# Softmax sums of two heads on four column quarters of PE, the halves of each sum added by DVE

## The chip, the cores and the metric

The kernel runs on one core of a Trainium2 chip. Five engines work side by side, each through its own instructions in order: PE (matrix multiply; weight loads stand apart in the profile as PEld), DVE (vector), ACT (activation functions and scaled copies), POOL (a second, slower vector engine) and SP, which here only issues DMAs. They wait for each other by semaphores. The metric is the device time of one execution in microseconds (us).

## The reference

Attention over 4 batches of 8 heads (576 tokens, head size 64, with rotary position), and after it a mixture of 8 experts whose gate is normalised by 8 rounds over rows and columns. The change is in the attention:

```python
scores = scale * np.matmul(q_rot, k_rot.transpose(0, 1, 3, 2))
scores = scores - np.max(scores, axis=-1, keepdims=True)
attn = np.exp(scores)
attn = attn / (np.sum(attn, axis=-1, keepdims=True) + 1e-09)
return np.matmul(attn, v).astype(np.float32)
...
logits = x @ w_gate
...
for e in range(E):
    h = np.maximum(x @ w1[e], 0.0)
    ye = h @ w2[e]
    out += P[:, e:e + 1] * ye
```

## The kernel before

Every fp32 operand of a matmul is split into a 16-bit high part and a 16-bit low part, and a product is the sum of three matmuls: high by high, high by low, low by high.

Attention goes over 16 pairs of heads. A pair's two heads lie on the two halves of the partitions (`HEADS`). For each pair PE computes the scores twice: `s_mm` (tile `s`) with queries on the partitions, from which DVE takes the maxima (`mraw`), and `t_mm` (tile `t`) with keys on the partitions, with the maxima subtracted by a further matmul. ACT makes the exponentials of `t` (tile `e`, fp32) and their high half (`eb`); POOL or DVE makes the low half.

`av_mm` is the step that this study is about. A pair has ten: two halves of the queries (288 columns each) by five blocks of keys, 160 in all. The product with V goes to the tile `av` (`po` in the code), the sum of the exponentials over the keys to the tile `as` (`pz`), as a product with a matrix of ones (`one16`). Head 0 uses columns 0 to 63 of PE and partitions 0 to 63 of the result, head 1 the other half, and the two matmuls of such a pair are issued one behind the other. A step has three pairs for `av` (V high by e high, V low by e high, V high by e low) and two for `as` (ones by e high, ones by e low), which accumulate into the same place. In the last block of keys, 64 long, the operands take 64 rows instead of 128.

`av_out` then has ACT copy `as` to `ss` (scaled by 2^12, with a small constant added) and `av` to `x`. 288 sums lie along one partition, and a reciprocal would be long there, so `sums_turn` turns them by way of DRAM, 32 times in all: rows of `ss` to `sd` (step 0), `sd` to the tile `s` with 64 partitions of 9 (step 1), then `av_recip` on DVE, back to `si` (step 2), and from there spread over the partitions as `rs` (step 3). `av_norm` multiplies `x` by `rs`; `x_half` splits the result into `xx`, the input of the experts.

The order of the whole part up to the first expert is made by a planner (`Plan`): each piece of work has an engine, an assumed time (table `US`: `av` for a step of `av_mm`, `r` for `av_recip`), a due time and the pieces it depends on, and the planner lays them out by simulated time. Every engine then runs its list in that order. Expert 0's first two blocks (lines 625 and 646, tile `g`) have late due times, and so fill PE where no attention step is ready. After attention come the gate and the rest of expert 0, up to about 600 us; the other seven experts run from there to the end.

Of the kernel before, what the change touches and what calls it, by code (L numbers as in the profile page):

```python
# [9 lines left out]
F32 = mybir.dt.float32  # L10
F16 = mybir.dt.float16
BF16 = mybir.dt.bfloat16
I32 = mybir.dt.int32
AF = mybir.ActivationFunctionType
ALU = mybir.AluOpType
# [4 lines left out]
P = 128  # L20
# [6 lines left out]
HS = S // 2  # L27
# [17 lines left out]
E_TOP = 10  # L45
# [9 lines left out]
AV_AT = ((3, 0, 0), (3, 0, 1), (4, 0, 2), (5, 0, 3), (6, 0, 4), (7, 1, 4), (8, 1, 0), (9, 1, 1), (10, 1, 2), (11, 1, 3))  # L55

US = dict(
    s=0.48, mx9=0.77, t=0.62, ex=0.84, eh=0.68, av=0.72, mx=1.36, gm=0.4, tt=1.05, ptt=1.4, sc=0.9, hi=0.78, lo=1.04,
    ad=1.12, pro=1.5, mp=0.7, mt=0.2, mr=0.95, n=0.82, d=2.3, r=0.25, x=0.95, xd=0.6, xh=0.44, xl=0.87, xld=0.6, v=0.85, vp=1.2,
    vh=0.84, vl=1.3, f=0.66, fh=0.62, fl=0.72, fc=0.62, w=1.25, wh=0.75, wl=1.0, lm=0.5, le=0.6, ld=6.5,  # L60
)
LATENCY = dict(pe=0.3, act=0.15, dve=0.15, pool=0.2, sp=0.0, none=0.0)
# [91 lines left out]
def attention_moe(ctx, tc, qk, v, trigs, eye, wg, w1, w2, out):  # L154
# [10 lines left out]
    pe, dve, act, pool, sp = nc.tensor, nc.vector, nc.scalar, nc.gpsimd, nc.sync  # L165
# [3 lines left out]
    def mkpool(name, bufs=1, **kw):  # L169
        return tc.alloc_tile_pool(name=name, bufs=bufs, reuse_waits="tile", **kw)  # L170

    dram = mkpool("dram", space=bass.MemoryType.DRAM)
# [6 lines left out]
    att = mkpool("att")  # L179
# [8 lines left out]
    xh, xl = xx[:, 0], xx[:, 1]  # L188
# [53 lines left out]
    idt = att.tile([P, 2, 192], BF16, name="idt")  # L242
    mask = eyes[:, 384:389]
    neg = att.tile([P, P], BF16, name="neg")
    one16 = att.tile([P, 64], F16, name="one16")
    ebias = att.tile([P, 1], F32, name="ebias")
    mbs = [att.tile([P, P], BF16, name=f"mb{i}") for i in range(2)]
    raw, vraw, Z, E, vhl, sc, vs, vmx, mraw, mps, R, avp, avx, inv9 = ({} for _ in range(14))
# [190 lines left out]
    def av_mm(p, qh, jt):  # L439

        first, last = (0, 4) if qh == 0 else (4, 3)
        if jt == first:
            avp[p, qh] = [ps_a.tile([P, 512], F32, tag=t, name=t)[:, 0:HS] for t in ("av", "as")]
        po, pz = avp[p, qh]
        vh, vl = vhl[p]
        e = E[9 * p + (4 if jt == 4 else 5 * qh + jt)]

        def side(j):
            if jt < 4:
                return vh[:, j, jt, :], vl[:, j, jt, :], one16, e[:, 0, j, :], e[:, 1, j, :]  # L450
            r = HEADS[j]
            return vh[r, j, 4, :], vl[r, j, 4, :], one16[r], e[r, 0, qh, :], e[r, 1, qh, :]

        ab = [side(j) for j in range(2)]
        for o, x, y, n in ((po, 0, 3, 0), (po, 1, 3, 1), (po, 0, 4, 2), (pz, 2, 3, 0), (pz, 2, 4, 2)):
            for j, r in enumerate(HEADS):
                pe.matmul(o[r], ab[j][x], ab[j][y], start=jt == first and n == 0, stop=jt == last and n == 2)  # L457

    def av_out(p, qh):
        po, pz = avp.pop((p, qh))  # L460
        x32 = att.tile([P, HS], F32, tag="x32", bufs=4, name="x32")
        s = att.tile([P, HS], F32, tag="ss", bufs=2, name="ss")
        act.activation(s, pz, AF.Copy, bias=1e-9 * 2.0 ** (E_TOP + 12), scale=2.0**12)
        act.copy(x32, po)  # L464
        avx[p, qh] = [x32, s]

    def sums_turn(p, qh, k):

        if k == 0:
            d = dram.tile([2, HS], F32, name=f"sd{p}{qh}")  # L470
            for j in range(2):
                sp.dma_start(out=d[j : j + 1, :], in_=avx[p, qh][1][64 * j : 64 * j + 1, :])
            inv9[p, qh] = d
        elif k == 1:
            t = att.tile([P, 9], F32, tag="s9", bufs=4, name="s9")[0:64]
            sp.dma_start(out=t, in_=inv9[p, qh].rearrange("j (a b) -> (j a) b", b=9))
            inv9[p, qh] = t
        elif k == 2:
            d = dram.tile([64, 9], F32, name=f"si{p}{qh}")
            sp.dma_start(out=d, in_=inv9[p, qh])  # L480
            inv9[p, qh] = d
        else:
            t = att.tile([P, HS], F32, tag="rs", bufs=2, name="rs")
            d = inv9.pop((p, qh)).rearrange("(j a) b -> j (a b)", j=2)
            for j in range(2):
                sp.dma_start(out=t[HEADS[j]], in_=d[j : j + 1, :].to_broadcast([64, HS]))
            avx[p, qh][1] = t

    def av_recip(p, qh):
        t = inv9[p, qh]  # L490
        dve.reciprocal(t, t)

    def av_norm(p, qh, e):
        x32, s = avx[p, qh]
# [184 lines left out]
    def pair_ops(p):  # L679
# [51 lines left out]
        for s, qh, jt in AV_AT:  # L731
            n = 9 * p + (4 if jt == 4 else 5 * qh + jt)
            name, a = f"AV.{p}.{qh}.{jt}", ("AV", (p, qh))
            first = jt == (0, 4)[qh]
            plan.add(
                name, ("pe", US["av"]), 9 * p + s + 0.3, lambda qh=qh, jt=jt: av_mm(p, qh, jt),
                [f"el.{n}", f"vl.{p}"] + ([done] if done else []), allocs=[a] if first else [],
                uses=([] if first else [a]) + [("E", n), ("vhl", p)],
            )
            done = name  # L740
        for j in range(2):
            x = ("xs", (p, j))
            add(f"n{j}", "act", "n", lambda j=j: av_out(p, j), [f"AV.{p}.{j}.{(4, 3)[j]}"], allocs=[x, ("ss", (p, j))], uses=[("AV", (p, j))])
            for k in range(4):
                if k == 2:
                    add(f"r{j}", "dve", "r", lambda j=j: av_recip(p, j), [f"d{j}1"], uses=[("s9", (p, j))])
                plan.add(
                    f"d{j}{k}.{p}", ("sp", US["d"]), at[f"d{j}"], lambda j=j, k=k: sums_turn(p, j, k),
                    [(f"n{j}.{p}", f"d{j}0.{p}", f"r{j}.{p}", f"d{j}2.{p}")[k]],
                    allocs=[[], [("s9", (p, j))], [], [("rs", (p, j))]][k],  # L750
                    uses=[[("ss", (p, j))], [], [("s9", (p, j))], []][k],
                )
            add(f"x{j}", flexible("x", "xd"), 0, lambda e, j=j: av_norm(p, j, e), [f"d{j}3"], uses=[x, ("rs", (p, j))])
            add(f"h{j}", "act", "xh", lambda j=j: x_half(p, j, 0), [f"x{j}"], uses=[x])
            add(f"l{j}", flexible("xl", "xld"), 0, lambda e, j=j: x_half(p, j, 1, e), [f"h{j}"], uses=[x])
# [118 lines left out]
    xd, xt_sb = {}, {}  # L874
# [421 lines left out]
```

## Time and profile before

| | |
|---|---|
| time, median of 3 runs | 1848.56 us (1846.24 to 1852.11) |
| the profiled execution's own time | 1848.74 us |
| its span, first to last instruction | 1846.9 us |
| PE busy in the span | 1750.3 us (95%) |
| DVE busy | 1192.4 us (65%) |
| ACT busy | 666.1 us (36%) |
| POOL busy | 471.5 us (26%) |

Rows that follow below are of five kinds. A table by stretch gives each engine's busy time with the number of instructions. A timeline gives start and length of merged instructions; the length of a matmul is modelled and includes its way through the array, so the distance between starts tells what it holds. A row by line or tile gives a group's count, busy time and mean, or its shortest, middle and longest duration. A wait is total us, times, longest us. A shape such as 128*64 in a matmul row is rows by columns of the array that it uses.

### The profile page before, as it was taken

The numbers are of one execution on the slowest core, as the hardware profiler recorded it, in microseconds if no ns is written. First come the engines' busy times: TensorE is split into PE (matmuls) and PEld (weight loads), VectorE is DVE, ScalarE is ACT, GpSimd is POOL, SyncE is SP. The second block draws the span as 40 slices with busy tenths as digits, with TensorE's granted clock in tenths as the row PEclk, the third lists the DMA queues.
The fourth block names the chain that finished last, engine by engine and source line by source line (L and its number), as shares of the span: only waits on it lengthen the run. The fifth ranks groups of instructions, "written<-read, shape, count | busy, mean of one in ns | idle before, by whom it ended". The sixth has DMA issues, their size and how long they took to land.

```text
span 1846.9 us, 32936 instructions
## 1 busy us (share of the span) xinstructions
PE 1750.3 (95%) x13920; PEld 1108.9 (60%) x13920; DVE 1192.4 (65%) x1909; ACT 666.1 (36%) x1121; POOL 471.5 (26%) x388
## 2 busy tenths in 40 slices
PE   3886899899999899999999999999999999999999
PEld 1544445555445566666666666666666666666665
DVE  8998899874680756564656564746475656656543
ACT  1774767677231422232223231313222222222221
POOL 2865667652221302020201010202021120101000
PEclk9998999999999999999999999999999999999999
DMA  5122212200110322131222222121222222222223
GB/s 195 59 89 87 72 56 66 91 15 15 52 64 17 108 76 93 57 103 60 95 75 75 86 69 82 68 92 67 83 69 81 80 81 69 72 89 72 78 80 92
DMA packets 45460, 140.06 MB, mean 76 GB/s; under 512 B 10304, under 2 KB 14720, under 8 KB 41216
## 3 DMA queue, kind: packets, MB, share of 16 engines
q1 hardware_dynamic: 45312, 137.96, 22.4%
q8 instruction: 109, 1.79, 0.4%
q14 instruction: 39, 0.32, 0.1%
HBM read 128.35 MB, written 9.58 MB: 75 GB/s over the span
## 4 chain that ended last, share of the span: by engine, by line
PE 74%; DVE 14%; DMA 5%; ACT 4%; issue 2%; POOL 1%; SPq 1%; DVEq 0%; POOLq 0%; ACTq 0%
PE m L1071 31%; PE m L1055 27%; PE g L646 4%; PE g L625 4%; PE s L379 2%; DVE mraw L380 2%; PE av L457 2%; DMA rs<-si 2%; PE t L424 1%; DMA wraw<-in_w 1%; DVE w1l L229 1%; DVE h L1096 1%; PE as L457 1%; DVE Z L229 1%; DMA si<-s 1%
## 5 line engine op out<-in xcount | busy, mean ns | idle before, releaser
L1071 PE MATMUL m<-w2h,h 128*128 128x512 f16 x2016 | 640.6, 379 | 0.0
L1071 PEld LDWEIGHTS <-h 128*128 128x128 f16 x3024 | 293.7, 98 | 302.4 <-issue 0.3
L1055 PEld LDWEIGHTS <-w1h 128*128 128x128 f16 x3920 | 369.7, 98 | 102.7 <-issue 12.3
L1071 PE MATMUL m<-w2l,h 128*128 128x512 f16 x1008 | 382.1, 379 | 0.0
L1055 PE MATMUL m<-ts,w1h 128*128 128x256 f16 (+1 forms) x2240 | 349.1, 262 | 2.7 <-DVE u L1087 2.7
L1087 POOL TENSOR_TENSOR c<-u,t 128x512 f32<-128x512 f32 (+1 forms) x70 | 82.6, 1180 | 814.6 <-DVE u L1087 722.2
L1055 PE MATMUL m<-ts,w1l 128*128 128x256 f16 (+1 forms) x1120 | 284.6, 262 | 0.0
L1092 ACT ACTIVATE h<-c 128x512 f16<-128x512 f32 (+1 forms) x210 | 117.2, 582 | 460.8 <-DVE c L1087 424.9
L1055 PE MATMUL m<-xx,w1h 128*128 128x256 f16 (+1 forms) x1680 | 263.0, 263 | 8.3 <-ACT m L1084 8.3
L1055 PE MATMUL m<-xx,w1l 128*128 128x256 f16 (+1 forms) x840 | 214.0, 263 | 0.0
L1096 DVE SCALAR_TENSOR_TENSOR h<-c,h 128x512 f16<-128x512 f32 (+1 forms) x210 | 143.1, 704 | 102.0 <-ACT h L1092 101.5
L1055 PEld LDWEIGHTS <-w1l 128*128 128x128 f16 x1960 | 192.0, 98 | 18.0
L435 POOL TENSOR_TENSOR eb<-e,eb 128x576 f16<-128x576 f32 x109 | 153.0, 1405 | 111.9 <-ACT eb L432 55.2
L1079 DVE SCALAR_TENSOR_TENSOR accA<-m,pp,accA 128x512 f32<-128x512 f32 x168 | 125.3, 746 | 74.7 <-PE m L1071 74.4
L428 ACT ACTIVATE e<-t,ebias,pc 128x576 f32<-128x576 f32 x144 | 119.7, 831 | 82.5 <-PE t L424 81.2
L379 PE MATMUL s<-Z 64*128 64x288 f16 (+1 forms) x960 | 92.3, 306 | 48.5 <-DVE mraw L380 42.2
L1079 DVE SCALAR_TENSOR_TENSOR accB<-m,pp,accB 128x512 f32<-128x512 f32 x84 | 63.0, 750 | 111.8 <-PE m L1071 111.8
L380 DVE TENSOR_REDUCE mraw<-s 128x2 f32<-128x576 f32 x144 | 107.3, 745 | 20.4 <-PE s L379 19.7
L1087 DVE TENSOR_TENSOR c<-m,u 128x512 f32<-128x512 f32 (+1 forms) x140 | 88.8, 634 | 38.7 <-PE m L1055 38.7
L1084 ACT COPY t<-m 128x512 f32<-128x512 f32 (+1 forms) x70 | 37.9, 541 | 205.0 <-PE m L1055 205.0
L432 ACT CAST eb<-e 128x576 f16<-128x576 f32 x144 | 96.6, 671 | 3.8
L457 PE MATMUL av<-eb,vh 128*64 128x288 f16 (+1 forms) x640 | 91.0, 301 | 6.9 <-ACT x L464 4.7
(148 smaller groups left out, 2205.4 us busy)
## 6 DMA issues: line engine op xcount, KB each, us to landing
ts<-xd SPq DMA_DIRECT2D x110, 512.0 KB
wraw<-in_w SPq DMA_DIRECT2D x28, 1024.0 KB
raw<-in_qk SPq DMA_DIRECT2D x32, 576.0 KB
ts<-xd SPq DMA_DIRECT2D x28, 256.0 KB
vraw<-in_v SPq DMA_DIRECT2D x4, 1280.0 KB
rs<-si SPq DMA_DIRECT2D x64, 72.0 KB
wraw<-in_w SPq DMA_DIRECT2D x8, 512.0 KB
xd<-ts SPq DMA_DIRECT2D x8, 512.0 KB
```

What stands on the lines that cost most here:

```text
L379: pe.matmul(po[j], zz[r, x, qc], zz[r, y, QH[kh]], start=n_ == 0, stop=n_ == 2)
L380: return lambda: dve.reduce_max(o, ps[:, :, 0:HS], axis=AX.X)
L428: act.activation(e32, ps[:, :, 0:HS], AF.Exp, bias=ebias, scale=sc[p][0])
L432: act.copy(E[g][:, 0], e32)
L435: engine[e].tensor_tensor(E[g][:, 1], e32, E[g][:, 0], op=ALU.subtract)
L457: pe.matmul(o[r], ab[j][x], ab[j][y], start=jt == first and n == 0, stop=jt == last and n == 2)
L1055: pe.matmul(live[bk][:, f * w : (f + 1) * w], x[:, a, i, fs], y[:, i], start=first and f == 0 and n == 0, stop=n == 5, skip_group_check=True,)
L1071: pe.matmul(po, x, y[:, ch], start=n == 0, stop=n == 11)
L1079: dve.scalar_tensor_tensor(o, pt.pop((th, j)), pp[e, hf][:, tt : tt + 1], o, op0=ALU.mult, op1=ALU.add)
L1087: engine[e_].tensor_tensor(temp(n, tag), live[x], live[y], **add)
L1092: act.activation(t[:, 0 : 2 * w], live[src], AF.Relu)
L1096: dve.scalar_tensor_tensor(f(hq[n][:, 1]), live[src], 0.0, f(hq[n][:, 0]), op0=ALU.max, op1=ALU.subtract)
```

## The change

`av_mm` keeps the three pairs for `av`. For `as`, the ones get 32 columns instead of 64, and the four products (high and low half of e, two heads) each get a quarter of the columns of their own: high half of head 0 and 1 on partitions 0 and 32, low half on 64 and 96. They are no longer accumulated into each other, so four rows leave `ss` instead of two, the tile `s` has two halves of 64x9, and `av_recip` adds them with the small constant in one scalar_tensor_tensor before the reciprocal. The factor 2^12 moves, as 2^-12, from the copy of the sums to the copy of `av`. In the planner's table `av` goes from 0.72 to 0.62 and `r` from 0.25 to 0.45.

```diff
-    s=0.48, mx9=0.77, t=0.62, ex=0.84, eh=0.68, av=0.72, mx=1.36, gm=0.4, tt=1.05, ptt=1.4, sc=0.9, hi=0.78, lo=1.04,
-    ad=1.12, pro=1.5, mp=0.7, mt=0.2, mr=0.95, n=0.82, d=2.3, r=0.25, x=0.95, xd=0.6, xh=0.44, xl=0.87, xld=0.6, v=0.85, vp=1.2,
+    s=0.48, mx9=0.77, t=0.62, ex=0.84, eh=0.68, av=0.62, mx=1.36, gm=0.4, tt=1.05, ptt=1.4, sc=0.9, hi=0.78, lo=1.04,
+    ad=1.12, pro=1.5, mp=0.7, mt=0.2, mr=0.95, n=0.82, d=2.3, r=0.45, x=0.95, xd=0.6, xh=0.44, xl=0.87, xld=0.6, v=0.85, vp=1.2,
...
-    one16 = att.tile([P, 64], F16, name="one16")
+    one16 = att.tile([P, 32], F16, name="one16")
...
-        for o, x, y, n in ((po, 0, 3, 0), (po, 1, 3, 1), (po, 0, 4, 2), (pz, 2, 3, 0), (pz, 2, 4, 2)):
+        for x, y, n in ((0, 3, 0), (1, 3, 1), (0, 4, 2)):
             for j, r in enumerate(HEADS):
-                pe.matmul(o[r], ab[j][x], ab[j][y], start=jt == first and n == 0, stop=jt == last and n == 2)
+                pe.matmul(po[r], ab[j][x], ab[j][y], start=jt == first and n == 0, stop=jt == last and n == 2)
+        for t in range(2):
+            for j in range(2):
+                g = slice(64 * t + 32 * j, 64 * t + 32 * j + 32)
+                pe.matmul(pz[g], ab[j][2], ab[j][3 + t], start=jt == first, stop=jt == last)
...
-        act.activation(s, pz, AF.Copy, bias=1e-9 * 2.0 ** (E_TOP + 12), scale=2.0**12)
-        act.copy(x32, po)
+        act.copy(s, pz)
+        act.activation(x32, po, AF.Copy, scale=2.0**-12)
...
-            d = dram.tile([2, HS], F32, name=f"sd{p}{qh}")
-            for j in range(2):
-                sp.dma_start(out=d[j : j + 1, :], in_=avx[p, qh][1][64 * j : 64 * j + 1, :])
+            d = dram.tile([2, 2 * HS], F32, name=f"sd{p}{qh}")
+            for g in range(2 * 2):
+                sp.dma_start(out=d[g // 2 : g // 2 + 1, g % 2 * HS : g % 2 * HS + HS], in_=avx[p, qh][1][32 * g : 32 * g + 1, :])
...
-            t = att.tile([P, 9], F32, tag="s9", bufs=4, name="s9")[0:64]
-            sp.dma_start(out=t, in_=inv9[p, qh].rearrange("j (a b) -> (j a) b", b=9))
+            t = att.tile([P, 2, 9], F32, tag="s9", bufs=4, name="s9")[0:64, 0:2]
+            sp.dma_start(out=t, in_=inv9[p, qh].rearrange("t (x b) -> x t b", b=9))
...
-        dve.reciprocal(t, t)
+        dve.scalar_tensor_tensor(t[:, 0], t[:, 0], 1e-9 * 2.0**E_TOP, t[:, 1], op0=ALU.add, op1=ALU.add)
+        dve.reciprocal(t[:, 0], t[:, 0])
```

Since the planner's table has changed, all engines get another order. On PE, in the fifth pair of heads, a step ended before (`as` is the tile of the sums, `one_106` the ones, `s` and `Z` the scores of another pair):

```order
L457 LDWEIGHTS one_106
L457 MATMUL as<-eb,one_106 64x288
L379 LDWEIGHTS Z
L379 MATMUL s<-Z 128x288
L379 LDWEIGHTS Z
L379 MATMUL s<-Z 128x288
```

At the same place of PE's list the changed kernel has (`vh` and `vl` are V's halves, `av` the product's tile):

```order
L461 LDWEIGHTS one_106
L461 MATMUL as<-eb,one_106 32x288
L457 LDWEIGHTS vh
L457 MATMUL av<-eb,vh 64x288
L457 LDWEIGHTS vh
L457 MATMUL av<-eb,vh 64x288
```

The sums now fill 32 partitions instead of 64, and the next step of `av_mm` follows directly, where scores stood between the two.

On DVE, in the first turn of sums, the list of before reads (`R` and `g` belong to the maxima, `wmx` to expert 0's weights):

```order
L405 TENSOR_SCALAR R<-g,eyes 128x64
L226 TENSOR_REDUCE wmx<-wraw 128x1
L491 RECIPROCAL s_673<-s_673 64x9
L380 TENSOR_REDUCE mraw<-s 128x2
L320 TENSOR_TENSOR raw<-raw 128x576
```

and that of the change, at the same place:

```order
L405 TENSOR_SCALAR R<-g,eyes 128x64
L226 TENSOR_REDUCE wmx<-wraw 128x1
L495 SCALAR_TENSOR_TENSOR s_678<-s_678 64x9
L496 RECIPROCAL s_678<-s_678 64x9
L380 TENSOR_REDUCE mraw<-s 128x2
L320 TENSOR_TENSOR raw<-raw 128x576
```

One instruction has come ahead of the reciprocal, and the maxima stand behind both.

On SP's queue, the second turn of the first pair was issued as

```order
L472 DMA sd_782<-ss 1x288 x2
L476 DMA s_822<-sd_782 64x9
L480 DMA si_875<-s_822 64x9
L486 DMA rs<-si_875 64x288 x2
L253 DMA raw<-in_qk 128x1152 x2
```

and is now issued, with the loads of a later pair's q and k (`raw`) inside it, as

```order
L476 DMA sd_835<-ss 1x288 x4
L480 DMA s_892<-sd_835 64x2x9
L253 DMA raw<-in_qk 128x1152 x2
L484 DMA si_944<-s_892 64x9
L490 DMA rs<-si_944 64x288 x2
```

Four rows go out instead of two, and the write-back of the reciprocals stands behind the loads.

## Rows read from the trace of the kernel before

**Rows 1.** Busy us (and instructions) of each engine by stretch, in us.
```profile
core 0: us, PE busy (x) PEld busy (x) DVE busy (x) ACT busy (x) POOL busy (x), PEclk, DMA share, GB/s
40.00:180.00 140.00, 105.56 (x1282) 67.30 (x1282) 128.19 (x194) 89.93 (x142) 94.73 (x70) 0.94 0.23 77
180.00:300.00 120.00, 110.77 (x1171) 59.48 (x1171) 107.05 (x160) 82.48 (x131) 73.58 (x57) 0.96 0.21 64
300.00:460.00 160.00, 151.71 (x1777) 85.92 (x1773) 118.04 (x193) 116.35 (x184) 86.84 (x67) 1.00 0.13 44
460.00:600.00 140.00, 137.26 (x744) 69.15 (x741) 73.52 (x159) 38.83 (x71) 29.07 (x24) 1.00 0.13 44
```

**Rows 2.** Expert 0's first matmuls, line 625: shortest, middle, longest ns; first, last start.
```profile
L625 PE MATMUL g<-xx,wh x130: 376/379/634, 180.1 to 476.2; 128*128 128x512 f16 x130
```

**Rows 3.** The chain that ended last, by line: 40 to 180, then 300 to 460 us.
```profile
by line: DVE mraw L380 10.9%; DVE Z L229 6.9%; DMA rs<-si 6.4%; issue 5.2%; DMA s<-sd 5.1%; DMA si<-s 5.1%; DVE wmx L226 4.9%; DVE vl L229 4.3%; DVE ctok L289 4.2%; ACT e L428 4.0%; DVE mb L390 3.8%; DVE wl L229 3.8%; PE s L379 3.7%; DVE mb
...
by line: PE av L457 14.6%; PE t L424 10.6%; PE g L625 10.2%; PE s L379 9.6%; PE as L457 7.4%; DMA rs<-si 6.2%; PE t L421 5.6%; PE g L646 4.1%; DMA sd<-ss 4.0%; DMA s<-sd 3.8%; DVE mraw L380 3.1%; DMA si<-s 3.1%; ACT e L428 2.0%; DVE vl L229
```

**Rows 4.** PE's waits, 40 to 180 us: total us, times, longest.
```profile
PE s L379 <- DVE mraw L380: 16.1, 12, 4.1
```

**Rows 5.** Tile as by stretch: PE busy, ACT busy (instructions), clock, DMA share, GB/s.
```profile
40.00:180.00 140.00, 22.22 (x200) 3.99 (x10) 0.94 0.23 77
180.00:300.00 120.00, 16.72 (x160) 3.22 (x8) 0.96 0.21 64
300.00:460.00 160.00, 28.60 (x280) 5.25 (x13) 1.00 0.13 44
```

**Rows 6.** Timeline of PE, two steps and what follows: start, length in us.
```profile
342.41 0.29 PE L457 MATMUL av<-eb,vh 128*64 128x288 f16 x2
...
343.39 0.41 PE L457 MATMUL as<-eb,one 128*64 128x288 f16 x4
343.73 0.54 PE L379 MATMUL s<-Z 64*128 64x288 f16 x6
```

**Rows 7.** Timeline of PE, from 128 to 64 columns.
```profile
186.86 0.59 PE L625 MATMUL g<-xx,wh 128*128 128x512 f16 x2
187.29 0.38 PE L625 MATMUL g<-xx,wl 128*128 128x512 f16 x1
187.60 0.31 PE L457 MATMUL av<-eb,vh 128*64 128x288 f16 x2
187.75 0.29 PE L457 MATMUL av<-eb,vl 128*64 128x288 f16 x2
```

**Rows 8.** Timeline of PE, from 64 to 128 columns.
```profile
456.20 0.41 PE L457 MATMUL as<-eb,one 128*64 128x288 f16 x4
456.54 0.60 PE L625 MATMUL g<-xx,wh 128*128 128x512 f16 x2
```

**Rows 9.** DVE's small operations: busy us, mean ns; durations of two of them.
```profile
L386 DVE TENSOR_TENSOR mm<-mraw 128x9 f32<-128x9 f32 x16 | 9.4, 589 | 0.6
L390 DVE TENSOR_TENSOR mb<-mm,mb 128x18 bf16<-128x18 f32 x16 | 8.3, 519 | 0.6
...
L390 DVE TENSOR_TENSOR mb<-mm,mb x16: 180/182/1326, 41.8 to 433.3; 128x18 bf16<-128x18 f32 x16
L491 DVE RECIPROCAL s<-s x32: 193/198/207, 66.5 to 465.7; 64x9 f32<-64x9 f32 x32
```

**Rows 10.** The turn of sums: row DMAs on SP (ns); DVE's wait; SP's wait.
```profile
L472 SPq DMA_DIRECT2D sd<-ss x64: 218/245/387, 59.0 to 461.0; - x64
...
DVE s L491 <- DMA s<-sd: 8.6, 3, 3.5
...
SPq L480 <- DVE s L491: 136.6, 32, 8.6
```

**Rows 11.** ACT's two copies of a turn: busy us, mean ns.
```profile
L463 ACT ACTIVATE ss<-as 128x288 f32<-128x288 f32 x32 | 12.9, 402 | 3.4 <-PE as L457 3.4
L464 ACT COPY x<-av 128x288 f32<-128x288 f32 x32 | 12.5, 391 | 0.0
```

More of the change, by code (lines that the diff above doesn't have):

```diff
@@ L479, in sums_turn @@
             d = dram.tile([64, 9], F32, name=f"si{p}{qh}")
-            sp.dma_start(out=d, in_=inv9[p, qh])
+            sp.dma_start(out=d, in_=inv9[p, qh][:, 0])
             inv9[p, qh] = d
```

## The prediction

> **What bounds the kernel now.** The changed lines run only in the attention part, the first 460 us. So I first asked which engine holds the clock there, with a table of busy time by stretch [rows 1]. Before 180 us DVE is busy 128.19 of 140 us and PE 105.56: DVE leads. From 180 to 300 us the two are level (PE 110.77, DVE 107.05 of 120). From 300 to 460 us PE is busy 151.71 of 160 and DVE 118.04, and from 460 to 600 PE is busy 137.26 of 140. The turn comes at 180.1 us, where the first matmul of expert 0 runs [rows 2]: from there PE has work with no deadline to put between attention steps, so what attention saves on PE becomes earlier filler and a shorter end. The chain that ended last says the same [rows 3]: in the first stretch it runs mostly over DVE lines and over the DMAs of the sums (rs, sd, si: 16.6% together), in the later one over PE's av, t, g, s and as. In the first stretch PE's largest wait is for DVE's maxima, 16.1 us [rows 4]. The time therefore has two prices: PE time counts after 180 us, DVE time before it.
>
> How many changed pieces lie in each stretch I read from the matmuls into `as` [rows 5]: 200, 160 and 280, at four a step, are 50, 40 and 70 of the 160 steps; the copies that empty `as`, 10, 8 and 13, are the turns of sums.
>
> **PE: what goes.** A step issues five pairs of matmuls, each pair on two halves of the columns. From 342.41 to 343.39 us two steps without a break start eight pairs in 0.98 us, 0.1225 us a pair [rows 6]. The change puts the two pairs of sums into one group of four. If the four run side by side as the two of a pair do, a step loses one pair: 160 x 0.1225 = 19.6 us in all, 110 x 0.1225 = 13.5 us after 180 us.
>
> **PE: what comes.** The sums now use 32 columns, the products 64, so the shape of the array in use changes inside each step. The trace shows what other changes of shape cost. Two pairs of `as` from 343.39 should end their turn at 343.39 + 0.245 = 343.635; the next shape, 64 rows by 128 columns, starts at 343.73: 0.095 us lost [rows 6]. Where only columns change, the same: two 512-column matmuls take 0.43 us from 186.86 to 187.29, so one more should free PE at 187.505, and the 64-column pair starts at 187.60 (0.095); its successor comes 0.15 later instead of 0.1225, as its weights were not ahead (0.025 more) [rows 7]. The way back, 64 to 128 columns, is 456.20 + 0.245 = 456.445 against 456.54 (0.095) [rows 8]. No row shows 64 to 32, so its bounds are 0 and 0.096 us. I take the upper: rows 7 and 8 change columns alone, and no neighbour of theirs is cheaper.
>
> The Trainium skill says it as a rule ("TensorEngine Tiling (Array Packing)", Tiling Modes, Key Properties): changing the tiling mode, not just the tile, drains the engine. By that rule, too, the upper bound holds; by the same page's speed-up of up to four for at most 32 columns alone, the step would just be a pair shorter. The rows on 64 and 128 columns agree with the first; none shows 32.
>
> Counting changes of shape down the two PE orders to the last step gives 443 before and 638 now: 195 more. One lies inside each of the 160 steps; the rest are mostly the 32 places where a step follows another directly, as in the shown piece, and PE must return from 32 to 64 columns. 195 x 0.096 = 18.7 us, and 32 x 0.025 = 0.8 us for weights: 19.5 us. Against 19.6 us saved, PE's sum is 0, and after 180 us (110 of 160) it is 0 as well.
>
> **DVE: what comes.** Each of 32 turns gets a scalar_tensor_tensor on 64x9 that adds the halves, ahead of the reciprocal. The reciprocal's row is no good price: it reads one tensor and always takes 193 to 207 ns. The nearest rows with two tensors in SBUF are 128x9 and 128x18: means 589 and 519 ns, and for the latter a median of 182 with a maximum of 1326 [rows 9]. The size of the data is nothing; something is sometimes waited for inside the instruction. Bounds: 0.18 and 1.33 us; I take 0.52, the mean of the row on the smallest operation that resembles it.
>
> The Trainium skill ("VectorE: DVE Perf Modes", Two Vector instructions with no wait between them) has an instruction with two SBUF tensors read the second through an interface shared with GpSimd; rows 9 agree, and POOL is busy 94.73 of 140 us in the first stretch. Priced by the reciprocal the edit would be 0.2 us a turn, by this row 0.52.
>
> Ten turns before 180 us are 5.2 us of DVE. DVE idles 8% there, partly in waits that the order can fill, so I count 3. Eight more up to 300 us are 4.2 us beside a PE as loaded; I count 1. The remaining 14 are hidden by PE (95% busy, DVE 74%). With the bounds: 10 x 0.18 = 1.8 us, nearly all hidden, up to 10 x 1.33 + 8 x 1.33 / 4 = 16 us.
>
> **The turn of sums.** Four row DMAs leave SP instead of two, 0.245 us each, so s lands 0.5 us later [rows 10]; the fetch of 64x2x9 has twice the pieces. DVE comes later than the data in 29 of 32 turns: it waited for them 3 times, 8.6 us. And SP waits for the reciprocal 136.6 us over 32 turns, 4.3 each, longer than a landing. So the half microsecond shows only where DVE stands waiting: 0.5 us in all, 1.5 if twice as many turns are late. Behind the waiting instruction stand DVE's maxima, and behind these PE's scores. In SP's new order two loads of q and k stand between the fetch and the write-back of the second turn, and wait there for a free buffer; the planner does this in few places, and four x buffers cover it.
>
> **ACT.** Scale and bias move from one copy to the other; with them it takes 402 ns, without 391 [rows 11]: nothing, as the two swap.
>
> **Sum.** 1848.74 us (the profiled execution, span 1846.9, 0.2 above the median of 1848.56) + 0 (PE) + 4 (DVE) + 0.5 (turn) = 1853.2: **1853 us**, +0.2%. A measurement of this kernel tells about 0.3%, 5.5 us, from no change.
>
> **Rivals.** (1) *Faster: 64 to 32 columns costs nothing.* If the 32-column groups count as parts of the 64-column halves, 13.5 us of the 19.6 arrive (the first 50 steps run where PE has slack): 1853 - 13.5 = 1839.5. For it: no row shows this pair of shapes. Against it: rows 6 to 8, one price for every pair. It decides where a change costs under 0.02 us: (0.096 - 0.02) x 134 changes after 180 us are the 10 us that part 1853 from 1843. Chance 0.20. (2) *The four don't run side by side*, but as two pairs, and the change doesn't do what it says: the saving is gone and the changes of shape stay: 1853 + 13.5 = 1866. Against it: two side by side are plain in rows 6. Chance 0.08. (3) *The two-tensor add meets POOL nearly each time* and costs 1.2 to 1.3 us: +14 us instead of 4, 1863. POOL is busy 68% of the first stretch, so it may. Chance 0.12. (4) *The new order*: the planner prices a step at 0.62 and puts 318 matmuls of expert 0 before the last step, not 270. PE stands idle 9 + 8 us from 180 to 460; if half of that is filled, 1853 - 8 = 1845. Chance 0.10. My own case has 0.50, alone 1847 to 1860.
>
> **Chances.** Faster by over 0.3% (below 1843): 0.16 of rival 1, 0.05 of my case, 0.04 of rival 4: 0.25. Slower (above 1854): 0.08 of rival 2, 0.11 of 3, 0.17 of my case: 0.36. Within: 0.39. The range 1839 to 1866 cuts about half of rivals 1 and 2 and the tail of 3, some 0.17.
>
> **What would show it.** In the new PE timeline the group of four should start 0.22 us after the last pair of products (0.12 would be rival 1), and what follows it 0.22 later (0.34 would be rival 2). PE's busy time to 460 us hardly shows it, since starts count. The row of the new add should have a mean near 0.52 with a median near 0.19. The first matmul of expert 0 should come 3 to 4 us later than 180.1. If that start comes no later, my DVE term is wrong; if the stretch from there to 600 us changes by over 5 us, my PE term is.

## The result and the profile after

The changed kernel takes 1865.67 us (median of 5 runs, 1863.75 to 1867.95), the kernel before 1849.23 (5 runs): a ratio of 1.0083, 95% interval 1.0060 to 1.0106. On 1849 us that is 15.3 us slower; the forecast was 4.5 slower, in a range that ended at 1866, 0.3 us above the measured time. The profiled execution took 1867.95 us, its span is 1866.1.

The table by stretch answers to [rows 1].

```profile
40.00:180.00 140.00, 106.58 (x1256) 61.39 (x1256) 124.48 (x185) 90.50 (x140) 97.27 (x72) 0.89 0.23 77
180.00:300.00 120.00, 108.16 (x1070) 51.40 (x1066) 105.94 (x167) 75.54 (x121) 65.40 (x52) 0.96 0.20 62
300.00:460.00 160.00, 146.08 (x1638) 72.23 (x1638) 126.68 (x200) 103.71 (x163) 79.79 (x65) 0.96 0.15 43
460.00:600.00 140.00, 137.94 (x907) 68.57 (x906) 91.91 (x184) 55.91 (x99) 32.41 (x25) 1.00 0.14 48
```

Up to 300 us no engine is much busier, and from 300 to 460 us only DVE is (126.68 us for 118.04). Yet in each of the first three stretches PE gets through fewer matmuls (1256 for 1282, 1070 for 1171, 1638 for 1777), and 907 instead of 744 are left for the fourth: attention advances more slowly. The granted clock is lower in the first stretch (0.89 for 0.94) and the third (0.96 for 1.00): PE was at 1.2 GHz for more of the time.

The group of four in PE's timeline, between the last pairs of products and what follows it:

```profile
274.22 0.29 PE L457 MATMUL av<-eb,vl 128*64 128x288 f16 x2
274.34 0.29 PE L457 MATMUL av<-eb,vh 128*64 128x288 f16 x2
274.56 0.31 PE L461 MATMUL as<-eb,one 128*32 128x288 f16 x4
274.80 0.39 PE L651 MATMUL g<-wh,hh 128*128 128x512 f16 x1
```

The pairs of products are 0.12 us apart, and the four start together 0.22 after the last: 0.0975 us beyond a pair's 0.1225. The change from 64 to 32 columns costs what the others cost. What follows starts 0.24 later, not 0.34 or more: the four do run side by side, and the way out costs 0.1175 us, 0.02 more than in [rows 8].

The new add and the reciprocal (shortest, middle, longest ns), expert 0's first matmuls, and the rows that leave `ss`, which answer to [rows 9], [rows 2] and [rows 10]:

```profile
L495 DVE SCALAR_TENSOR_TENSOR s<-s x32: 150/156/1360, 66.8 to 500.0; 64x9 f32<-64x9 f32 x32
L496 DVE RECIPROCAL s<-s x32: 206/207/208, 67.9 to 500.2; 64x9 f32<-64x9 f32 x32
...
L630 PE MATMUL g<-xx,wh x320: 272/379/634, 185.3 to 591.1; 128*128 128x512 f16 x128, 128*128 128x256 f16 x32
...
L476 SPq DMA_DIRECT2D sd<-ss x128: 212/249/439, 60.1 to 494.9; - x128
```

The add's usual length is 0.156 us and its longest 1.36; its mean, in the view by line, is 0.466 us:

```profile
L495 DVE SCALAR_TENSOR_TENSOR s<-s 64x9 f32<-64x9 f32 x32 | 14.9, 466 | 4.9 <-DMA s<-sd 4.9
```

Expert 0 starts 5.2 us later than in [rows 2], where 3 to 4 were forecast. The last sums of attention reach `ss` and leave it at 494.9 us, where [rows 10] has 461.0; 48 more matmuls of expert 0 come ahead of them in the new order, 48 x 0.215 = 10 us of the 34. The other 24 us were not taken apart.

### The profile page after: what moved, and what is told of

Same layout as the page of the kernel before. It is cut to its first block, busy times and chain, and to the rows that moved or that the text cites. A ratio compares the mean times of both kernels' runs of the same rounds, so it can differ in the third digit from the quotient of the medians.

```text
span 1866.1 us, 33078 instructions
## 1 busy us (share of the span) xinstructions
PE 1763.8 (95%) x13920; PEld 1090.6 (58%) x13920; DVE 1215.3 (65%) x1944; ACT 666.9 (36%) x1121; POOL 463.1 (25%) x385
## 4 chain that ended last, share of the span: by engine, by line
PE 60%; DVE 3%; ACT 1%; issue 1%; DMA 1%; POOL 0%
PE m L1076 32%; PE m L1060 28%; DVE w1l L229 1%; DVE h L1101 1%; DMA wraw<-in_w 1%; DVE accA L1084 0%; ACT h L1097 0%; DVE wmx L226 0%; DVE c L1092 0%; ACT w2h L233 0%; ACT accA L876 0%; POOL c L1092 0%; DVE u L1092 0%; ACT w1h L233 0%; ACT m L1089 0%
## 5 line engine op out<-in xcount | busy, mean ns | idle before, releaser
L1092 POOL TENSOR_TENSOR c<-u,t 128x512 f32<-128x512 f32 (+1 forms) x70 | 81.9, 1171 | 815.2 <-DVE u L1092 721.8
L435 POOL TENSOR_TENSOR eb<-e,eb 128x576 f16<-128x576 f32 x102 | 143.0, 1404 | 102.5 <-ACT eb L432 74.7
L457 PE MATMUL av<-eb,vh 128*64 128x288 f16 (+1 forms) x640 | 95.2, 312 | 6.6 <-POOL eb L435 3.6
```

The lines of the kernel that those rows point to most:

```text
L435: engine[e].tensor_tensor(E[g][:, 1], e32, E[g][:, 0], op=ALU.subtract)
L457: pe.matmul(po[r], ab[j][x], ab[j][y], start=jt == first and n == 0, stop=jt == last and n == 2)
L1092: engine[e_].tensor_tensor(temp(n, tag), live[x], live[y], **add)
```

## The experiments

Theories: A, the changes of shape on PE (with the add and the turn) cost what the result shows in any order; B, the planner's new order does; C, PE's time is covered and the longer turn of sums costs it; D and E, two readings of why an add of 9 numbers a partition costs so much. Ratios are to runs of the kernel before on the same chip, with the 95% interval; us are that ratio on 1849. The ratio is not that of the two medians, so the two can differ by a microsecond or two.

**The old order.** The changed kernel with the planner's old table.

```diff
-    s=0.48, mx9=0.77, t=0.62, ex=0.84, eh=0.68, av=0.62, mx=1.36, gm=0.4, tt=1.05, ptt=1.4, sc=0.9, hi=0.78, lo=1.04,
+    s=0.48, mx9=0.77, t=0.62, ex=0.84, eh=0.68, av=0.72, mx=1.36, gm=0.4, tt=1.05, ptt=1.4, sc=0.9, hi=0.78, lo=1.04,
```

(and `r` from 0.45 back to 0.25). Expected: 

> The changed kernel with the planner's old table (av 0.72, r 0.25), so that every engine runs the order of before, with the new group of four and the new add in their places. Theory A (the changes of shape, the add and the turn cost what the result shows, whatever the order): 1860 to 1868 us. Theory B (the planner's new order, made with a step priced too low, costs most of it): 1849 to 1854 us. Changes of shape counted down PE's order to the last step: 626, against 443 before.

Measured: 1861.88 us, 1.0068 (1.0055 to 1.0080), +12.6 us. The order is not the main cause.

**The new order alone.** The kernel before with the new table (`av` 0.62, `r` 0.45). Expected: 

> The kernel before with the new table alone (av 0.62, r 0.45): old matmuls, old turn, the order of the changed kernel. Theory A: 1849 us, within 4. Theory B: 1860 to 1868 us.

Measured: 1851.95 us, 1.0014 (1.0005 to 1.0024), +2.6 us. Theory B holds for a sixth of the loss.

**A pair less, nothing else.**

```diff
-        for o, x, y, n in ((po, 0, 3, 0), (po, 1, 3, 1), (po, 0, 4, 2), (pz, 2, 3, 0), (pz, 2, 4, 2)):
+        for o, x, y, n in ((po, 0, 3, 0), (po, 1, 3, 1), (po, 0, 4, 2), (pz, 2, 3, 3)):
...
-                pe.matmul(o[r], ab[j][x], ab[j][y], start=jt == first and n == 0, stop=jt == last and n == 2)
+                pe.matmul(o[r], ab[j][x], ab[j][y], start=jt == first and n in (0, 3), stop=jt == last and n in (2, 3))
```

Expected: 

> The kernel before without the pair that sums the low halves of the exponentials (it leaves the low half out of the softmax sums): a step of four pairs, no change of shape inside, old turn, old table. This is what the change would give if a change of shape cost nothing. If PE's time counts after 180 us as predicted: 110 x 0.1225 = 13.5 us less, 1832 to 1839 us. If PE's time is hidden in attention: 1846 to 1850 us.

Measured: 1845.69 us against 1848.56 before, 0.9993 (0.9980 to 1.0007): -1.3 us, not to be told from nothing. This fell out against the prediction: 19.6 us less of PE's work, of which 13.5 after 180 us, bring at most 4.

**All in quarters.** No change of shape inside a step: V's products too go out in groups of four.

```diff
-            for j, r in enumerate(HEADS):
-                pe.matmul(po[r], ab[j][x], ab[j][y], start=jt == first and n == 0, stop=jt == last and n == 2)
+            for j in range(2):
+                for h in range(2):
+                    g = slice(64 * j + 32 * h, 64 * j + 32 * h + 32)
+                    pe.matmul(
+                        po[g], ab[j][x][:, 32 * h : 32 * h + 32], ab[j][y], start=jt == first and n == 0,
+                        stop=jt == last and n == 2,
+                    )
```

Expected: 

> The changed kernel with the old table, and the products with V as well in quarters of the columns: each pair of 64 columns becomes four matmuls of 32 columns, so a step is four groups of four and the shape doesn't change inside it. Theory A (the change inside the step is what eats the saved pair): the pair saved after 180 us is 13.5 us, the turn and the add still cost some 5: 1836 to 1846 us. If groups of four don't run side by side, or sixteen issues hold PE up: over 1866 us. If the loss sits in the turn and the add instead: 1855 us and more.

Measured: 1861.95 us, 1.0078 (1.0065 to 1.0092), +14.4 us. Taking the changes of shape out of the steps brought nothing, where theory A allowed 1846 at most; theory A falls, and the loss is to be looked for in the turn.

**Changes of shape alone.** The sums accumulate as before, by two groups of four in place of two pairs.

```diff
-                pe.matmul(o[r], ab[j][x], ab[j][y], start=jt == first and n == 0, stop=jt == last and n == 2)
+                for g in [r] if x < 2 else [slice(64 * j + 32 * h, 64 * j + 32 * h + 32) for h in range(2)]:
+                    pe.matmul(o[g], ab[j][x], ab[j][y], start=jt == first and n == 0, stop=jt == last and n == 2)
```

Expected: 

> The kernel before with the two pairs for the sums issued as two groups of four matmuls of 32 columns that accumulate as before: five turns of PE a step as before, plus a change of shape inside each step; old turn, old table. PE's own bill is 183 changes of 0.096 us in and some 0.02 more on the way out: 20 us. Theory A (changes of shape carry the loss): 1860 to 1868 us. Theory C (PE's time is covered in attention, as the run without a pair showed, and the longer turn of sums with its add on DVE carries the loss): 1848 to 1854 us.

Measured: 1859.51 us, 1.0052 (1.0040 to 1.0064), +9.6 us. The time lies just below theory A's range and well above theory C's. More work on PE does cost, where less brought nothing: about half of the 20 us added arrives.

**The turn alone.** Matmuls as before, four rows, the larger fetch, the add (a scalar_tensor_tensor, which here reads two tensors).

```diff
-            d = dram.tile([2, HS], F32, name=f"sd{p}{qh}")
-            for j in range(2):
-                sp.dma_start(out=d[j : j + 1, :], in_=avx[p, qh][1][64 * j : 64 * j + 1, :])
+            d = dram.tile([2, 2 * HS], F32, name=f"sd{p}{qh}")
+            for g in range(2 * 2):
+                sp.dma_start(out=d[g % 2 : g % 2 + 1, g // 2 * HS : g // 2 * HS + HS], in_=avx[p, qh][1][32 * g : 32 * g + 1, :])
...
-        dve.reciprocal(t, t)
+        dve.scalar_tensor_tensor(t[:, 0], t[:, 0], 1e-9 * 2.0 ** (E_TOP + 12), t[:, 1], op0=ALU.add, op1=ALU.add)
+        dve.reciprocal(t[:, 0], t[:, 0])
```

Expected: 

> The kernel before with the new turn alone: matmuls as before, four rows out of ss, the fetch of 64x2x9, and the add on DVE (the two halves are here two copies of the whole sum, the scale is half). Old table. Theory C: 1858 to 1864 us. Theory A: 1849 to 1853 us.

Measured: 1859.40 us, 1.0060 (1.0048 to 1.0072), +11.1 us: theory C.

**The rows alone.** The same without the scalar_tensor_tensor. Expected: 

> As the run with the new turn alone, without the add on DVE: four row DMAs and the larger fetch, the reciprocal of one half. If the DMAs carry theory C's loss: 1855 to 1862 us. If DVE's add carries it: 1848 to 1851 us.

Measured: 1850.15 us, 1.0010 (1.0001 to 1.0019), +1.8 us.

**The add alone.** The old turn, with a scalar_tensor_tensor that adds a tile of zeros.

```diff
-        dve.reciprocal(t, t)
+        dve.scalar_tensor_tensor(t, t, 0.0, zero9[0:64], op0=ALU.add, op1=ALU.add)
+        dve.reciprocal(t, t)
```

Expected: 

> The kernel before with a scalar_tensor_tensor on 64x9 ahead of each reciprocal, which adds a tile of zeros: the turn's DMAs as before. By the rows of the changed kernel it takes 0.47 us on average, 32 times, 15 us of DVE. If DVE's add carries theory C's loss: 1855 to 1862 us. If the DMAs carry it: 1848 to 1852 us.

Measured: 1859.81 us, 1.0052 (1.0039 to 1.0065), +9.6 us. The add carries most of the turn's price: rows and add measured apart make 1.8 + 9.6 = 11.4, against 11.1 measured together, within the intervals.

**The turn with a reduction.** The add as an operation that reads one tensor.

```diff
-        dve.scalar_tensor_tensor(t[:, 0], t[:, 0], 1e-9 * 2.0 ** (E_TOP + 12), t[:, 1], op0=ALU.add, op1=ALU.add)
-        dve.reciprocal(t[:, 0], t[:, 0])
+        u = att.tile([P, 9], F32, tag="u9", bufs=4, name="u9")[0:64]
+        dve.reduce_sum(u, t.rearrange("p t b -> p b t"), axis=AX.X)
+        inv9[p, qh] = u
+        dve.reciprocal(u, u)
```

Expected: 

> The run with the new turn alone, with the add done by a tensor_reduce over the two halves into a tile of its own, which reads one tensor, instead of the scalar_tensor_tensor on two. Theory D (the add's price is DVE's wait for POOL inside an instruction that reads two tensors): the add falls from 0.39 to about 0.17 us, and with it 11 us of loss to some 5: 1852 to 1856 us. Theory E (the price is that of any further instruction between the landing and the reciprocal): 1858 to 1862 us.

Measured: 1855.45 us, 1.0049 (1.0035 to 1.0064), +9.1 us. In its trace, and in that of the add alone:

```profile
L492 DVE TENSOR_REDUCE u<-s x32: 155/158/168, 66.4 to 471.1; 64x9 f32<-64x18 f32 x32
```

```profile
L492 DVE SCALAR_TENSOR_TENSOR s<-s,zero x32: 149/154/1381, 68.7 to 476.3; 64x9 f32<-64x9 f32 x32
```

The two operations have the same usual length; only the one that reads two tensors is ever long, up to 1.38 us. In the run with the add alone each of the ten adds over 0.2 us started while a tensor_tensor of POOL was running and ended 0.02 us after it, as here:

```profile
338.52 1.27 POOL L436 TENSOR_TENSOR eb<-e,eb 128x576 f16<-128x576 f32 x1
```

```profile
338.98 0.83 DVE L492 SCALAR_TENSOR_TENSOR s<-s,zero 64x9 f32<-64x9 f32 x1 [4.61 <-DMA s<-sd]
```

(A bracket holds how long the engine stood idle before, and what ended it.) The other 22 met no instruction of POOL, one that started after them, or the last 0.12 us of one. Eleven of the 32 reductions started in the middle of a tensor_tensor of POOL, and took 0.155 to 0.167 us. That part of theory D is shown. But the time fell by only 2 us of the expected 6 against the run with the new turn, inside what the intervals allow for nothing (1855.45 lies in theory D's range only because this chip's runs of before are faster, 1846.60).

**The whole change with a reduction**, in the old order (the same edit in the changed kernel). Expected: 

> The whole change in the old order (old table), with the add done by a tensor_reduce. The same run with the scalar_tensor_tensor was 12.6 us over before. Theory D: 5 to 7 us less than that, 1854 to 1858 us. Theory E: 1860 to 1863 us.

Measured: 1855.76 us, 1.0044 (1.0031 to 1.0056), +8.1 us, 4.5 less than with the scalar_tensor_tensor. Each of the two differences, 2.0 and 4.5, is uncertain by over 3 us. By their mean the wait for POOL is some third of the add's price, a rough share; the rest stays with an instruction of 0.16 us that waits for nothing inside. Theory D and theory E each hold in part. Whether an instruction elsewhere in DVE's list would cost as much was not run.

**The matmuls of the change alone.** The kernel before with the change's matmuls: old order, old turn, the scale and constant of before. Against the changed kernel, in the turn:

```diff
-            for g in range(2 * 2):
-                sp.dma_start(out=d[g // 2 : g // 2 + 1, g % 2 * HS : g % 2 * HS + HS], in_=avx[p, qh][1][32 * g : 32 * g + 1, :])
+            for j in range(2):
+                sp.dma_start(out=d[j : j + 1, :], in_=avx[p, qh][1][32 * j : 32 * j + 1, :])
...
-        dve.scalar_tensor_tensor(t[:, 0], t[:, 0], 1e-9 * 2.0**E_TOP, t[:, 1], op0=ALU.add, op1=ALU.add)
```

Expected: 

> The matmuls of the change alone, in the old order: three pairs and one group of four, but only the two rows of the high halves leave ss, by the old turn without an add (it leaves the low halves out of the softmax sums). Prediction's PE bill: saved 19.6, changes of shape 17.6, their weights and way out some 4: +2 us of PE work, and so 1848 to 1852 us. If a change of shape costs more than its gap (by other instructions that come late, or by the clock): 1854 to 1860 us.

Measured: 1848.71 us against 1846.60 before, 1.0009 (1.0000 to 1.0019), +1.7 us.

**All in quarters, old turn.** Expected: 

> As the run before in this list, with the products with V in quarters as well, so that no shape changes inside a step: four turns of PE, old turn, low halves left out of the sums. If PE's work is what counts, as in the run without a pair: 1844 to 1848 us. If sixteen matmuls of 32 columns cost something of their own (their issue, or the clock): 1850 us and more.

Measured: 1846.75 us, 0.9996 (0.9984 to 1.0007), -0.7 us. Sixteen matmuls of 32 columns a step cost nothing that the time shows, and bring nothing. In the trace their groups of four start 0.12 us apart (223.35, 223.47, 223.60), as pairs do. With the turn's 11.1 us this makes 10.4, where the run with both had 14.4; that these 4 us are more than chance is not shown, and what they would be stays open.

## Why the prediction was right, and where its sizes were off

The forecast of 1853 was short by 12.5 us, and the prediction's own case, 1847 to 1860, does not hold the time. That the whole range does, by 0.3 us, is luck: its end of 1866 is the time of rival 2, whose mechanism is not there. What failed is the step that hides the add on DVE, above all behind PE from 300 us on: 4 us were let through for it, and it costs 9 to 10.

The bill adds up from parts that were run by themselves: matmuls 1.7, turn 11.1 (of which rows 1.8, so 9.3 for the add), order 2.6: 15.4 us, against 15.3 measured. In the old order the first two make 12.8, against 12.6. Each part is uncertain by some 2 us and the whole by 4, so that they agree to a tenth is chance.

**PE's sum: right within 3 us of PE's work.** It was forecast at 0. Of its parts, 64 to 32 columns costs 0.0975 us in the trace, the bound that was taken; the four run side by side; the way out is dearer by 0.02, 3 us over 160 steps, which the sum left out. The run with the matmuls alone, +1.7, agrees, but it is a weak test, since 19.6 us of PE's work less moved the time by only 1.3. Rivals 1 and 2 are refuted by the rows of the group of four. The Trainium skill has a change of tiling mode drain the engine ("TensorEngine Tiling (Array Packing)", Key Properties). The trace agrees for 64 to 32 columns, with the 0.0975 us.

The prediction's own sign would have called its PE term wrong: expert 0's first matmul comes 5.2 us later, the profiled execution ends 19.2 us later, so the stretch behind that matmul changes by 14 us, not by under 5. The run with the matmuls alone shows that the sign was badly chosen: what the add and the order cost comes out in that stretch too.

**"PE time counts after 180 us": wrong, and without effect on the sum, since the sum was 0.** To see where PE counts, the same matmuls (every matmul of line 421 has its fellow in each trace, since the order is the same) were set side by side, one execution of each kernel. First the start in the kernel before, then how much later the same matmul starts, us:

```
before               44.1  182.0  240.4  305.9  330.7  339.2  369.5  409.6  452.4
a pair less          +0.8    0.0   -0.5   -1.0   -1.0   -1.1   -2.5   -2.4   -5.0
changes of shape     +1.2   +1.4   +1.7   +3.4   +4.2   +6.7   +7.5   +9.1  +11.7
the add alone        +2.0   +4.9   +3.6   +3.8   +5.2   +8.3   +9.5  +10.9  +10.8
the rows alone       -0.1   +1.4   +1.0   +1.6   +1.9   +2.1   +3.6   +3.8   +3.6
```

A pair less gains 1.1 us up to 339 us, and 3.9 in the 113 us from there. So work taken from PE pays from about 340 us, not from 180. Work put on PE costs earlier: changes of shape lose 5.3 us from 182 to 339 us and 5.0 behind it. The table by stretch could have told the first, cut at another place. In the trace of before:

```profile
180.00:340.00 160.00, 147.21 (x1603) 80.89 (x1602) 141.77 (x208) 109.80 (x174) 106.09 (x80) 0.97 0.23 74
340.00:460.00 120.00, 115.27 (x1341) 64.51 (x1340) 83.32 (x145) 89.02 (x141) 54.32 (x44) 1.00 0.08 24
```

DVE is busy 89% up to 340 us and 69% after it; my cut at 300 averaged the two to 74%. The 5 us gained by 452 us are those of one execution (1843.01 us, 5.7 below that of before), which lies low among its own runs; over the 12 runs 1.3 are left. Six of the 12 had a mean granted clock of 0.988 to 0.990 and took 1843.7 us on average, the other six 0.985 or 0.986 and 1847.9, where the kernel before has 0.989 to 0.993. Whether a lower clock takes back part of what the pair saves, or only goes with the longer runs, was not tested.

**The add: its length nearly right, its overlap wrong.** Its length was forecast at 0.52 us by the mean of the nearest two-tensor row, and is 0.466 (0.38 to 0.41 in the runs in the old order). The forecast let 4 of its 16.6 us count: 3 of the ten turns before 180 us, 1 of the eight to 300, nothing of the rest. Measured alone it costs 9.6 us, where its busy time is 12.0. By the table it takes 4.9 us by 182 (3 forecast), gives 1 back by 306, and takes 7 more between 306 and 410, where it was written off as hidden. The largest jump, 3.1 us between 331 and 339, shows how. SP's queue in the run with the add alone:

```profile
324.20 0.47 SPq L481 DMA_DIRECT2D si<-s  x1
325.91 1.08 SPq L487 DMA_DIRECT2D rs<-si  x2
327.65 0.85 SPq L254 DMA_DIRECT2D raw<-in_qk  x2
329.47 0.33 SPq L258 DMA_DIRECT2D vraw<-in_v  x1
329.85 0.58 SPq L473 DMA_DIRECT2D sd<-ss  x2
336.29 0.45 SPq L477 DMA_DIRECT2D s<-sd  x1
```

and DVE's timeline there, with PE's first wait behind it:

```profile
333.63 0.75 DVE L321 TENSOR_TENSOR raw<-raw 128x576 f32<-128x576 f32 x1
338.98 0.83 DVE L492 SCALAR_TENSOR_TENSOR s<-s,zero 64x9 f32<-64x9 f32 x1 [4.61 <-DMA s<-sd]
339.84 0.21 DVE L493 RECIPROCAL s<-s 64x9 f32<-64x9 f32 x1
339.97 0.69 DVE L381 TENSOR_REDUCE mraw<-s 128x2 f32<-128x576 f32 x1
```

```profile
340.72 0.91 PE L380 MATMUL s<-Z 64*128 64x288 f16 x6 [3.43 <-DVE mraw L381]
...
343.85 0.39 PE L648 MATMUL g<-wh,hh 128*128 128x512 f16 x1
```

The same place in the kernel before:

```profile
319.15 0.47 SPq L480 DMA_DIRECT2D si<-s  x1
320.85 1.08 SPq L486 DMA_DIRECT2D rs<-si  x2
322.03 1.68 SPq L253 DMA_DIRECT2D raw<-in_qk  x2
323.76 0.42 SPq L257 DMA_DIRECT2D vraw<-in_v  x1
324.23 0.69 SPq L472 DMA_DIRECT2D sd<-ss  x2
331.08 0.45 SPq L476 DMA_DIRECT2D s<-sd  x1
```

```profile
332.87 0.21 DVE L491 RECIPROCAL s<-s 64x9 f32<-64x9 f32 x1 [3.36 <-DMA s<-sd]
```

```profile
333.74 0.54 PE L379 MATMUL s<-Z 64*128 64x288 f16 x6 [1.69 <-DVE mraw L380]
...
335.46 0.39 PE L646 MATMUL g<-wh,hh 128*128 128x512 f16 x1
```

In both, the sums' rows leave SP right behind the loads of the next pair and of V, and the fetch follows only 6 to 7 us later; DVE stands at the head of its list waiting for it. The write-back of an earlier turn (324.20 for 319.15) and all behind it on SP come 5.1 to 5.7 us later with the add. DVE waits 4.61 us, where it waited 3.36 before, the add takes 0.83 on top, the maxima come behind both, and PE's scores wait 3.43 us for them, where they waited 1.69. These are 1.7 of the 3.1 us. The other 1.4 come behind the wait: the scores start 7.0 us later than before, the next matmul of expert 0 (tile `g`) 8.4 later. In between the granted clock is 0.50, which is 1.2 GHz, and six matmuls take 0.91 us instead of 0.54. The first row is of the run with the add, the second of before, at the same place:

```profile
340.40:343.80 3.40, 3.08 (x24) 1.73 (x23) 3.40 (x5) 1.09 (x2) 0.00 (x0) 0.50 0.11 25
```

```profile
333.70:337.10 3.40, 3.33 (x39) 2.12 (x38) 3.40 (x4) 2.10 (x4) 1.17 (x2) 1.00 0.11 27
```

Here DVE's time is not spent beside PE's work but in front of it, and PE then goes on at half its clock. The place makes other delays longer too: with the changes of shape alone, without an add, 2.5 us are lost between 331 and 339 (PE waits 2.64 us there, and the clock falls to 1.2 GHz behind it). The prediction has no term for the clock. From 340 to 460 us it was 1.00 before (above), 0.97 with the add alone (first row) and 0.96 in the changed kernel (second):

```profile
340.00:460.00 120.00, 113.38 (x1303) 63.91 (x1304) 87.97 (x156) 85.41 (x136) 54.93 (x44) 0.97 0.09 25
340.00:460.00 120.00, 108.99 (x1223) 54.42 (x1220) 93.71 (x148) 78.72 (x123) 59.78 (x50) 0.96 0.14 42
```

By an estimate from these rows, 0.03 and 0.04 of 120 us are at most 3.6 and 4.8 us of PE's work. No run tells this part from the rest.

**The turn: 0.5 forecast, 1.8 measured** (0.2 to 3.5), its upper bound of 1.5 within the interval. **The order: left out of the sum, and named only as a gain (rival 4); it is a loss of 2.6.** Why it loses was not tested; the planner's price of 0.62 for a step is 0.1 below the old one, while a step of the change takes no less PE time than before.

**Rival 3** had the right engine, with +14 us for an add that costs 9 to 10, but its mechanism, that the add meets POOL nearly each time, is not what the rows show: half of the adds take no more than 0.156 us. The chance for slower, 0.36, stood behind the one for no change, 0.39, because my own case was too small by the add.

## What to carry to other kernels

Before a pair of matmuls is saved, take one out of the kernel, however wrong the sum, and see what it is worth: here 19.6 us of PE's work were worth 1.3 and at most 4, though PE is busy 95%. An instruction added behind a DMA's landing, on an engine that runs in order and is busy 90%, is to be priced at first as if it stood on the path: here it cost 9.6 us for 12.0 of its own, four fifths, where a quarter was forecast. Behind the longer wait PE's clock fell as well, which the price of the wait does not show. And a stretch over which busy shares are averaged should end where the work changes, not at a round number.

## What the hardware showed that was not expected

Leaving a shape of 32 columns costs 0.1175 us where leaving one of 64 costs 0.095. A tensor_reduce on 64x18 took 155 to 168 ns in all 32 cases. A scalar_tensor_tensor of the same size took 149 to 1381, beside the same work of POOL; when it was long, it ended 0.02 us after the tensor_tensor of POOL in which it had started. The reciprocal of 64x9 right behind such an operation on its own input takes 207 ns instead of 199. In the run with the matmuls alone the clock granted to PE from 40 to 180 us fell to 0.85, from 0.94 before, yet the matmul of line 421 that started at 182.0 us before came only 0.55 us later: a lower clock cost little in a stretch where DVE leads.

```profile
40.00:180.00 140.00, 113.59 (x1274) 63.18 (x1274) 125.69 (x191) 89.29 (x141) 95.07 (x70) 0.85 0.23 77
```
